# Reordering the Strassen sums of a fused linear-attention and gated-MLP kernel between VectorE and GpSimd

## The chip, the core and the metric

The kernel runs on one core of a Trainium2 chip. The metric is the device time of one launch in microseconds; before the change it is 294.11 us (median of three runs, 294.11 to 294.32). The traced execution spans 292.1 us, and every time of day below ("at 107.95") is microseconds from the start of that span.

The engines are PE (TensorE: matmuls; its weight loads are listed as PEld), DVE (VectorE), ACT (ScalarE), POOL (GpSimd) and SP (which issues the DMAs). Each works through its own queue of instructions strictly in the order of the program, and waits for the others through semaphores.

## What is computed

```
q_s = softmax(q, over head_dim)          # 8 batches, 8 heads, 576 rows, 64 wide
k_s = softmax(k, over the rows)
attn = q_s @ (k_s^T @ v)                 # per head
x = attn, heads side by side             # 4608 x 512
g, val = x @ w_gate, x @ w_val           # 512 -> 1536
out = (gelu(g) * val) @ w_out            # 1536 -> 512, float32
```

## The kernel before

**Blocks.** The work goes through nine blocks of 512 rows: the main rows of batches 0 to 6, then block 8 (the 64 left-over rows of all batches), then block 7. Each block makes `xt` (the attention output, transposed), then `ht` (the hidden rows, `gelu(g)*val`, twelve chunks of 128), then the output product. The attention of the following batch is threaded into the block.

**Two levels of Strassen products.** In blocks 1 and later the output product (`out_strassen`, L755) multiplies `ht` with `w_out` in seven products instead of eight, by way of sums of quarters of `ht`. With `a11, a21, a12, a22` for the quarters (`sum_h`, L576), the four sums are

- 1: `sh[1] = a21 + a22`
- 2: `sh[2] = sh[1] - a11`
- 3: `a21 = a11 - a21`, in place in `ht`
- 4: `s4 = a12 - sh[2]`

Product 5 reads sum 1, product 6 sum 2, product 3 sum 4, product 7 sum 3. `sum_h(j0, j1, which, eng)` does the listed sums for one pair of chunks (`j` = 0, 1 or 2; 128x512 f16) on DVE or on POOL. From block 2 on the first-level products of x with the weights are done the same way for chunks in pairs: `pair_step(b, xt, k, i)` is step `i` (1 to 4) of pair `k`. Step 2 ends with an `add` on DVE (L670), step 3 with another `add` and a `final` (gelu on ACT, multiply on DVE), and `upper` (gelu on ACT, multiply on POOL, L676) closes the pair's other half. Step 4 of a pair accumulates on the bank `pga` that step 3's addition reads. `sum_x` (L613, POOL) makes the sums `xs` of `xt` that these products read. The weights' sums are made once: `sum_wgv` (L595) and, later, chunk by chunk, `sum_w1` (L604).

**What sets the order.** An order written by hand. In blocks 2 and 3 it is the string `FOUR` (L634): `0.1` is step 1 of pair 0, `8g` and `8v` are plain gate and value products of chunk 8 (`half`, L643), and a word such as `s0` or `u0` calls what `plan` has under that name. `s0`/`s1` and `u0`/`u1` are the sums of `ht` for pair 0 and pair 1. `at(b, kind, i, ...)` fills the plan and `ride(b, kind, i)` runs it; `NS` 0 to 4 are places inside `out_strassen`. `u1` is run by `out_strassen` itself, after product 1's fourth chunk (L796). Block 1 has no pairs; its sums for the first four chunks come from `SUMS` (L733), run after the chunk with that number.

**The places that matter.** In `out_strassen`: a snapshot `snap` is a copy of a PSUM bank to SBUF (L775 on ACT, L777 on DVE) that must be taken before the next product accumulates on the same bank; `add` (L783) adds a bank to a snapshot into the output rows. `psa` carries products 1, 6, 7 and 4 in turn, `psc` carries 5 and 3, `psb` carries 2. So product 3 waits for the snapshot of product 5, product 7 for that of product 6, and product 4 for the addition of product 7. After product 6 the attention of the next block is threaded in (`unit_kv4`, L340, and `unit_x4`, L426, whose copies into `xt` are on ACT and DVE).

Of the kernel before, what the change touches and what calls it, by code (L numbers as in the profile page):

```python
# [18 lines left out]
def kernel(  # L19
# [29 lines left out]
    NO = NFI // 2  # L49
# [30 lines left out]
    def big(shape, dt, name, hold=False, seed=False):  # L80
        tag = ring.pop(next(i for i, x in enumerate(ring) if x in full) if seed else 0)
        t = ps_big.tile(shape, dt, name=name, tag=tag)
        words = 1
        for n in shape[1:]:
            words *= n
        (full.add if words == 512 and shape[0] == 128 and dt == f32 else full.discard)(tag)
        if hold:
            held[id(t)] = (t, tag)
        else:
            ring.append(tag)  # L90
        return t

    def let_go(t):
        ring.append(held.pop(id(t))[1])
# [481 lines left out]
    def sum_h(j0, j1, which, eng="dve"):  # L576
        step = 1 if j0 in (0, 4) and j1 < NO + (j0 > 0) else NO // 2
        js, ks = slice(j0, j1, step), slice(NO + j0, NO + j1, step)
        a11, a21 = ht[:, js, 0:256], ht[:, js, 256:512]
        a12, a22 = ht[:, ks, 0:256], ht[:, ks, 256:512]  # L580
        s1, s2 = sh[1][:, js], sh[2][:, js]
        for i in which:
            o, a, b, op = {1: (s1, a21, a22, ALU.add), 2: (s2, s1, a11, ALU.subtract),
                           3: (a21, a11, a21, ALU.subtract),
                           4: (s4[:, js], a12, s2, ALU.subtract)}[i]
            (nc.gpsimd if eng == "pool" else nc.vector).tensor_tensor(out=o, in0=a, in1=b, op=op)  # L586
# [32 lines left out]
    def product_gv(i, ps, xt, k, first):  # L619
        lo, hi = slice(k * P, (k + 1) * P), slice((k + NO // 2) * P, (k + NO // 2 + 1) * P)  # L620
        xs = xs_b[xt is st.get((B - 1, "xt"))]
        for t, w, nm in ((0, wv_sb, "v"), (1, wg_sb, "g")):
# [8 lines left out]

    FOUR = ("a 7g l 7v n 0.1 6.1 0.2 6.2 0.3 6.3 m p 10g 0.4 6.4 1.1 t 10v 1.2 s0 8g u0 1.3 8v 1.4 2.1"  # L634
            " 11g 2.2 11v 2.3 s1")
    FIVE = ("a 8g l 8v n m 0.1 6.1 0.2 6.2 0.3 6.3 0.4 1.1 p 6.4 7.1 t 1.2 7.2 1.3 s0 7.3 2.1 1.4 u0 11g 2.2"
            " y 7.4 11v 2.3 s1")
# [1 line left out]
           " 8.2 2.3 s1 8.3 2.4")  # L639
    steps = {b: (SIX if b >= B - 1 else FIVE if b > 3 else FOUR).split() for b in range(2, B + 1)}  # L640
    live = {}
# [88 lines left out]
            if late:  # L730
                late()

    SUMS = {9: (0, 4, (1, 2)), 10: (0, 4, (3, 4))}  # L733

    def product(i, ps, first, ts=(0, 1), js=range(NO)):
        for j in js:
# [12 lines left out]
    def get_x(b):  # L749
        return get_xt(b) if b < B else xtr  # L750

    def last_js(b):
        return (NO - 2 if b < 2 else NO // 2 - 1, NO)

    def out_strassen(b, last):  # L755
        yo = [yop.tile([P, 2, C], f32, name="yo", tag="yo") for _ in range(2)]
        c = (slice(0, 256), slice(256, 512))
        ps, tiles_ = {}, {}

        def get(nm):  # L760
            if last:
                tiles_[nm] = [big([P, 256], f32, "ps" + nm, True) for _ in range(2)]
                ps[nm] = [x for x in tiles_[nm]]
            else:
                tiles_[nm] = [big([P, 2, 256], f32, "ps" + nm, True)]
                ps[nm] = [tiles_[nm][0][:, t] for t in range(2)]

        def parts(nm):
            return [(0, ps[nm][0]), (1, ps[nm][1])] if last else [(slice(0, 2), tiles_[nm][0])]

        def snap(nm, act=False):
            sn = ffn.tile([P, 2, 256], f32, name="sn", tag="gl")
            for n, (t, src) in enumerate(parts(nm)):
                if n or act:
                    nc.scalar.activation(out=sn[:, t], in_=src, func=ACTF.Copy, scale=1.0 / _H_SCALE)  # L775
                else:
                    nc.vector.tensor_scalar(out=sn[:, t], in0=src, scalar1=1.0 / _H_SCALE,  # L777
                                            scalar2=None, op0=ALU.mult)
            return sn

        def add(nm, sn, half, col):
            for t, src in parts(nm):
                nc.vector.scalar_tensor_tensor(  # L783
                    out=yo[half][:, t, c[col]], in0=src, scalar=1.0 / _H_SCALE,
                    in1=sn[:, t], op0=ALU.mult, op1=ALU.add)

        js = (0, 1, 2, 3, 4, 5) if b < 2 else (0, 3, 1, 4, 2, 5)
        get("a")
        four = 1 < b < B - 1
        cut = 3 if four else 4  # L790
        product(1, ps["a"], True, js=js[:cut])
        if four:
            pair_step(b, get_x(b), NO // 2 - 1, 4)
            product(1, ps["a"], False, js=js[cut:4])
        ride(b, NS, 0)
        if b < 4:  # L796
            ride(b, PR, "u1")
        if b >= B - 1:
            pair_step(b, get_x(b), NFI - NO // 2 - 1, 4)
        get("b")  # L800
        product(1, ps["a"], False, js=js[4:])
        if b > 1:
            s1 = snap("a", True)
        ride(b, PR, "e")
        sum_h(*last_js(b), (1,))
        if b > 3:
            ride(b, PR, "u1")
        sum_h(*last_js(b), (2,))
        if b < 2:
            s1 = snap("a")  # L810
        product(2, ps["b"], True, js=js)
        add("b", s1, 0, 0)
        for x in tiles_["b"]:
            let_go(x)
        sum_h(*last_js(b), (4,), "pool" if b > 1 else "dve")
        get("c")
        product(5, ps["c"], True, js=js)
        sum_h(*last_js(b), (3,), "pool" if b > 1 else "dve")
        s5 = snap("c", b == B or b == B - 2)
        ride(b, NS, 1)  # L820
        product(6, ps["a"], False, js=js)
        s2 = snap("a", b == B or b == B - 2)
        ride(b, NS, 2)
        cut = NO - 1 if 1 < b < B - 2 else NO
        product(3, ps["c"], False, js=js[:cut])
        if cut < NO:
            product(7, ps["a"], False, js=js)
            add("a", s5, 1, 1)
            product(3, ps["c"], False, js=js[cut:])
        add("c", s2, 0, 1)  # L830
        for x in tiles_["c"]:
            let_go(x)
        store_rows(b, 0, yo[0])
        if last:
            finish_last(b, ps["a"], yo[1], s5)
            return
        if cut == NO:
            product(7, ps["a"], False, js=js)
            add("a", s5, 1, 1)
        ride(b, NS, 4)  # L840
        if b == B:
            go_on(B - 1, get_x(B - 1), 1)
        product(4, ps["a"], False, js=js)
        nc.scalar.activation(out=yo[1][:, :, c[0]], in_=tiles_["a"][0], func=ACTF.Copy,
                             scale=1.0 / _H_SCALE)
        let_go(tiles_["a"][0])
        store_rows(b, 1, yo[1])
# [16 lines left out]
    def store_rows(b, half, yo):  # L864
        if b < B:
            store(nc.sync, yo.rearrange("p n c -> p (n c)"), b, 2 * half, 2 * half + 2)
            return
        for t in range(2):
            for j in range(2):
                o = 2 * (2 * half + t) + j  # L870
                nc.sync.dma_start(
                    out=out[o * S:(o + 1) * S, :].rearrange("(m n) c -> m n c", n=NT)[:, 0, :],
                    in_=yo[j * 64:(j + 1) * 64, t, :])
# [71 lines left out]
    FI, NS, PR = range(3)  # L945
    plan = {}

    def at(b, kind, i, *fns):
        plan.setdefault((b, kind, i), []).extend(fns)

    L = lambda f, *a: (lambda: f(*a))
# [35 lines left out]
    for i, x in enumerate(("g1", "v1", "g2", "v2", "g4", "v4")):  # L987
        at(0, FI, 5 + i, L(sum_wgv, x[0], int(x[1])))
    at(0, FI, NFI - 2, L(sum_w, 1))
    at(1, NS, 1, L(sum_wgv, "g", 3))  # L990
    at(1, NS, 2, L(sum_wgv, "v", 3))
    for b in range(2, B):
        n = b + 1
        if n < B:
# [13 lines left out]
    for b in range(2, B - 1):  # L1008
        n = b + 1
# [6 lines left out]
    for b in range(2, B + 1):  # L1016
        for j in range(NO // 2 - 1):
            at(b, PR, f"s{j}", L(sum_h, j, NO, (1,)))
            if j and b > 3:
                at(b, PR, f"u{j}", L(sum_h, j, NO, (2, 3, 4)))  # L1020
            else:
                at(b, PR, f"s{j}", L(sum_h, j, NO, (3,), "pool"))
                at(b, PR, f"u{j}", L(sum_h, j, NO, (2,)), L(sum_h, j, NO, (4,), "pool"))
    for b, kind, i, dk, x in ((1, FI, 6, 0, 1), (1, FI, 6, 0, 2), (1, FI, 6, 0, 4), (1, FI, 9, 0, 3),
                              (2, NS, 1, 1, 1), (2, NS, 1, 1, 2), (3, NS, 2, 1, 4), (3, NS, 2, 1, 3),
                              (4, NS, 2, 2, 1), (4, NS, 2, 2, 2), (6, NS, 1, 2, 4), (6, NS, 2, 2, 3)):
        at(b, kind, i, L(sum_w1, x, NO + dk, "pool" if b < 3 else "dve"))


    def ride(b, kind, i):  # L1030
        for fn in plan.get((b, kind, i), []):
            fn()

    for b in order:
# [11 lines left out]
        for fi in range(fi0, NFI if b < 2 else 0):  # L1046
            ffn_fi(xt, fi, b == 1 and fi == 7)
            ride(b, FI, fi)
            if b > 0 and fi in SUMS:
                sum_h(*SUMS[fi])  # L1050
        if b == 0:
# [44 lines left out]
```

The softmax here doesn't subtract the row's maximum and nothing guards it: scores larger than these inputs give would overflow.

## Time and profile before

| view | what it says |
|---|---|
| page, busy time | PE 281.8 us, 96% of the span; DVE 78%, POOL 69%, ACT 68% |
| page, clock | TensorE's granted clock is at 9 or more tenths in every slice |
| chain that ended last | 87% of the span on PE, 4% DVE, 4% POOL |
| sums of h on DVE (L586), groups by shape | 22 of `sh<-sh,ht` at a mean of 603 ns; 22 of `sh<-ht` at 441 ns; six of `s<-ht,sh` at 418 ns |
| sums of h on POOL (L586) | 16 of `ht<-ht` at 1197 ns, 16 of `s<-ht,sh` at 1172 ns |
| chunk sums of the weights (L611) | POOL 1156 to 1602 ns, DVE 916 and 1150 ns |
| blocks in the trace | block 1's output product 70.7 to 82.2; block 2 from 82.2, its output product 101 to 112.6; block 3 from 112.6, its output product 132.2 to 143.8; block 4 from 143.8 |

A matmul is pipelined: one of 256 columns lasts 272 ns in the records, but twelve in a row leave PE after 1.31 us, 0.109 us each, and four of 512 columns after 0.86 us. PE's lost time is therefore read from the starts: where a group of matmuls begins, plus its number times this pitch, is where the next could begin. The idle time in square brackets in a timeline is shorter than that loss, because it is counted from the modelled end of the last matmul.

### The profile page before, as it was taken

The page shows a single profiled execution, that of the slowest core. Times are in us where ns is not written, and L with a number is a line of the kernel's source. Part 1 is how long each engine was busy: PE and PEld are TensorE (multiplying, and loading weights), DVE is VectorE, ACT ScalarE, POOL GpSimd, SP SyncE. Part 2 cuts the span into 40 slices and gives each one's busy share as a digit, 9 for nine tenths or more (in the row PEclk, how much of TensorE's full clock was granted, in tenths as well). Part 3 has the DMA queues.
Part 4 walks back from the last instruction along what each step waited for, and adds up shares of the span by engine and source line. Part 5 has one row for each costly group of instructions (what it writes and reads, how often), then busy time and mean ns, then how long its engine had stood idle before and what let it go on. Part 6 is the DMA issues. An engine that isn't in the chain of part 4 may idle for free.

```text
span 292.1 us, 6496 instructions
## 1 busy us (share of the span) xinstructions
PE 281.8 (96%) x2497; PEld 207.5 (71%) x2497; DVE 229.2 (78%) x426; ACT 198.1 (68%) x332; POOL 200.2 (69%) x184
## 2 busy tenths in 40 slices
PE   3999999999999999999999999999999999999994
PEld 1444445445777786768688878887888888888883
DVE  2954888868997678669988889887889779938992
ACT  3763367785697688766887698769774477537650
POOL 1567746986478589976996689759975476283640
PEclk9999999999999999999999999999999999999999
DMA  6999999998059903990189318921240110033003
GB/s 217 374 381 388 400 392 390 354 342 236 3 165 375 183 2 137 345 239 2 72 271 323 74 74 274 312 67 53 93 83 19 72 75 0 3 73 73 2 0 144
DMA packets 54622, 51.72 MB, mean 177 GB/s; under 512 B 18496, under 2 KB 50496, under 8 KB 54592
## 3 DMA queue, kind: packets, MB, share of 16 engines
q1 hardware_dynamic: 52864, 49.49, 54.1%
q10 hardware_dynamic: 1728, 1.84, 1.9%
q8 instruction: 19, 0.31, 0.4%
q14 instruction: 11, 0.09, 0.1%
HBM read 37.75 MB, written 9.44 MB: 162 GB/s over the span
## 4 chain that ended last, share of the span: by engine, by line
PE 87%; DVE 4%; POOL 4%; DMA 2%; ACT 1%; issue 1%; POOLq 0%; ACTq 0%
PE pga L629 21%; PE psa L745 12%; PE psg L471 11%; PE psv L471 10%; PE pgc L629 10%; PE psc L745 6%; PE pgb L629 5%; PE psy L539 4%; PE psb L745 2%; DMA qt<-in_q_dram 2%; DVE sh L586 2%; PE pskv L347 2%; POOL s L586 1%; POOL v L186 1%; PE psx L434 1%
## 5 line engine op out<-in xcount | busy, mean ns | idle before, releaser
L629 PEld LDWEIGHTS <-wgv_sb 128*128 128x128 f16 x560 | 54.3, 98 | 11.2 <-issue 0.8
L471 PEld LDWEIGHTS <-wgv_sb 128*128 128x128 f16 x304 | 29.5, 98 | 30.3 <-issue 0.7
L248 POOL TENSOR_TENSOR eq<-eq,rrq 128x640 f16<-128x640 f16 (+1 forms) x27 | 34.8, 1306 | 11.3 <-DVE rrq L240 7.3
L745 PEld LDWEIGHTS <-ht 128*128 128x128 f16 x384 | 36.6, 98 | 7.8 <-issue 2.5
L471 PE MATMUL psg<-xt,wgv_sb 128*128 128x512 f16 x152 | 41.1, 379 | 0.0
L471 PE MATMUL psv<-xt,wgv_sb 128*128 128x512 f16 x152 | 41.0, 379 | 0.0
L676 POOL TENSOR_TENSOR ht<-eq 128x512 f16<-128x512 f32 x17 | 21.7, 1274 | 22.4 <-ACT eq L674 22.4
L629 PE MATMUL pga<-xs,wgv_sb 128*128 128x256 f16 x232 | 34.5, 272 | 0.2 <-DVE cc L670 0.2
L586 POOL TENSOR_TENSOR s<-ht,sh 128x512 f16<-128x512 f16 x16 | 18.7, 1172 | 13.9 <-DVE sh L586 13.9
L656 ACT ACTIVATE glq<-pgb 128x256 f32<-128x256 f32 x35 | 13.3, 381 | 21.1 <-PE pgb L629 14.4
L657 DVE SCALAR_TENSOR_TENSOR ht<-pga,glq 128x256 f16<-128x256 f32 x35 | 14.8, 422 | 14.2 <-ACT glq L656 14.0
L586 POOL TENSOR_TENSOR ht<-ht 128x512 f16<-128x512 f16 x16 | 19.2, 1197 | 8.7 <-DVE sh L586 8.7
L476 ACT ACTIVATE gl<-psg 128x512 f32<-128x512 f32 x24 | 13.8, 598 | 16.6 <-PE psg L471 16.5
L186 POOL CAST v<-vt 128x640 f16<-128x640 f32 x26 | 19.1, 777 | 8.1 <-PE pskv L347 6.4
L477 DVE SCALAR_TENSOR_TENSOR ht<-psv,gl 128x512 f16<-128x512 f32 x24 | 16.0, 686 | 10.0 <-PE psv L471 8.2
L686 ACT COPY pgb<-pga 128x512 f32<-128x512 f32 x35 | 20.4, 582 | 5.1 <-PE pga L629 4.8
L745 PE MATMUL psa<-tw,ht 128*128 128x256 f16 x192 | 23.4, 272 | 0.1
L666 ACT ACTIVATE snq<-pga 128x512 f32<-128x512 f32 x35 | 20.9, 600 | 3.5 <-PE pga L629 3.2
L210 ACT ACTIVATE ek<-kt 128x1280 f16<-128x1280 f32 (+1 forms) x11 | 19.1, 1748 | 6.1 <-DMA kt<-in_k_dram 4.2
L676 POOL TENSOR_TENSOR ht<-cc 128x512 f16<-128x512 f32 x16 | 20.4, 1272 | 2.8 <-ACT cc L674 2.8
L238 DVE TENSOR_REDUCE rq<-eq 128x20 f32<-128x1280 f16 (+1 forms) x12 | 17.2, 1432 | 4.4 <-ACT eq L210 4.4
L745 PEld LDWEIGHTS <-sh 128*128 128x128 f16 x192 | 18.7, 98 | 2.3
(173 smaller groups left out, 685.2 us busy)
## 6 DMA issues: line engine op xcount, KB each, us to landing
out_dram<-yo SPq DMA_DIRECT2D x15, 512.0 KB, 3.4
kt<-in_k_dram SPq DMA_DIRECT2D x7, 640.0 KB, 9.0
vt<-in_v_dram SPq DMA_DIRECT2D x7, 640.0 KB, 5.9
qt<-in_q_dram SPq DMA_DIRECT2D x7, 640.0 KB, 7.7
qt<-in_q_dram SPq DMA_DIRECT2D x8, 512.0 KB, 8.4
wost<-in_moe_w_out_dram SPq DMA_DIRECT2D x6, 512.0 KB, 7.9
kt<-in_k_dram SPq DMA_DIRECT2D x6, 512.0 KB, 9.6
vt<-in_v_dram SPq DMA_DIRECT2D x6, 512.0 KB, 6.5
```

Of the source, the lines that this page charges most:

```text
L186: nc.gpsimd.tensor_copy(out=dst, in_=src)
L210: nc.scalar.activation(out=dst[:, n0:NC, h0 * D:h1 * D].rearrange(o, d=D, **({"t": 2} if b >= QUAD else {})), in_=heads(tiles[(nm, b)], b, ...
L238: nc.vector.reduce_sum(rq, e, axis=mybir.AxisListType.X)
L248: (nc.gpsimd if eng == "pool" else nc.vector).tensor_tensor(out=e, in0=e, in1=rrq.unsqueeze(-1).to_broadcast((P, n, 2, D)), op=ALU.mult)
L471: nc.tensor.matmul(ps, w[:, ci, fi * P:(fi + 1) * P], xt[:, ci, :], start=(ci == 0), stop=(ci == HP - 1))
L477: nc.vector.scalar_tensor_tensor(out=ht[:, fi, :], in0=psv, scalar=_H_SCALE, in1=gl, op0=ALU.mult, op1=ALU.mult)
L586: (nc.gpsimd if eng == "pool" else nc.vector).tensor_tensor(out=o, in0=a, in1=b, op=op)
L629: nc.tensor.matmul(ps[:, t], a, x, start=(first and t == 0 and c == 0), stop=(c == 1), skip_group_check=True)
L666: nc.scalar.activation(out=sn, in_=ps, func=ACTF.Copy, scale=_H_SCALE)
L676: (nc.vector if k == NFI - NO // 2 - 1 else nc.gpsimd).tensor_tensor(out=ht[:, k:k + NO // 2 + 1:NO // 2, 256:512], in0=cc[:, :, 0], in1=c ...
L686: nc.scalar.copy(out=pb, in_=pa)
L745: nc.tensor.matmul(ps[t], a, w, start=(first and j == js[0] and (t == ts[0] or ps[t].tensor is not ps[ts[0]].tensor)), stop=(j == js[-1]), ...
```

## The change

It moves sums, and adds or removes none. There are five edits.

1. In `FOUR` (blocks 2 and 3) the word `s0` moves from ahead of `8g 1.3` to behind them, and `u0` from ahead of `1.3` to behind `8v`. Pair 0's sums on DVE then stand behind step 1.3's addition. The order of the matmuls stays.
2. In blocks 2 and 3 pair 1's sum 4 goes from POOL to DVE (in `u1`, next to sum 2), and pair 1's sum 3 stays on POOL but is queued later, under the new name `r1`, behind pair 2's sum 4.
3. In block 1 sum 4 of chunks 0 to 3 moves from after chunk 10 to after chunk 11, so that it stands behind chunk 11's multiply on DVE.
4. In block 1 the weights' sum `g3` moves from the place after product 5 to the place after product 6, beside `v3`, so that both stand behind the second snapshot.
5. In block 2 two chunk sums of the weights go from POOL to DVE, and from the place after product 5 to the place after product 6.

Its aim is to free PE's short waits at the addition of step 1.3, at the snapshots and at `xs`.

```diff
-    FOUR = ("... 6.4 1.1 t 10v 1.2 s0 8g u0 1.3 8v 1.4 2.1"
+    FOUR = ("... 6.4 1.1 t 10v 1.2 8g 1.3 s0 8v u0 1.4 2.1"
             " 11g 2.2 11v 2.3 s1")
...
-    SUMS = {9: (0, 4, (1, 2)), 10: (0, 4, (3, 4))}
+    SUMS = {9: (0, 4, (1, 2)), 10: (0, 4, (3,)), 11: (0, 4, (4,))}
...
         sum_h(*last_js(b), (4,), "pool" if b > 1 else "dve")
+        ride(b, PR, "r1")
         get("c")
         product(5, ps["c"], True, js=js)
...
-    at(1, NS, 1, L(sum_wgv, "g", 3))
-    at(1, NS, 2, L(sum_wgv, "v", 3))
+    at(1, NS, 2, L(sum_wgv, "g", 3), L(sum_wgv, "v", 3))
...
             else:
-                at(b, PR, f"s{j}", L(sum_h, j, NO, (3,), "pool"))
-                at(b, PR, f"u{j}", L(sum_h, j, NO, (2,)), L(sum_h, j, NO, (4,), "pool"))
+                if j:
+                    at(b, PR, "r1", L(sum_h, j, NO, (3,), "pool"))
+                    at(b, PR, "u1", L(sum_h, j, NO, (2, 4)))
+                else:
+                    at(b, PR, "s0", L(sum_h, j, NO, (3,), "pool"))
+                    at(b, PR, "u0", L(sum_h, j, NO, (2,)), L(sum_h, j, NO, (4,), "pool"))
...
-                              (2, NS, 1, 1, 1), (2, NS, 1, 1, 2), (3, NS, 2, 1, 4), (3, NS, 2, 1, 3),
+                              (2, NS, 2, 1, 1), (2, NS, 2, 1, 2), (3, NS, 2, 1, 4), (3, NS, 2, 1, 3),
...
-        at(b, kind, i, L(sum_w1, x, NO + dk, "pool" if b < 3 else "dve"))
+        at(b, kind, i, L(sum_w1, x, NO + dk, "pool" if b < 2 else "dve"))
```

More of the change, by code (lines that the diff above doesn't have):

```diff
@@ L630, in product_gv @@
                                  skip_group_check=True)
-    FOUR = ("a 7g l 7v n 0.1 6.1 0.2 6.2 0.3 6.3 m p 10g 0.4 6.4 1.1 t 10v 1.2 s0 8g u0 1.3 8v 1.4 2.1"
+    FOUR = ("a 7g l 7v n 0.1 6.1 0.2 6.2 0.3 6.3 m p 10g 0.4 6.4 1.1 t 10v 1.2 8g 1.3 s0 8v u0 1.4 2.1"
             " 11g 2.2 11v 2.3 s1")
```

## The prediction

> **What bounds the kernel now.** I read the page first, then PE's waits, then the timeline around each.
>
> ```profile
> PE 281.8 (96%) x2497; PEld 207.5 (71%) x2497; DVE 229.2 (78%) x426; ACT 198.1 (68%) x332; POOL 200.2 (69%) x184
> PE 87%; DVE 4%; POOL 4%; DMA 2%; ACT 1%; issue 1%; POOLq 0%; ACTq 0%
> ```
>
> PE is the bound: 96% busy, 87% of the chain. No edit removes a matmul, so all that can be won is time in which PE stands still. The view of PE's waits names where:
>
> ```profile
> PE psc L745 <- POOL s L586: 0.5, 2, 0.3
> PE pgc L629 <- POOL xs L617: 0.3, 1, 0.3
> PE pga L629 <- DVE cc L670: 0.2, 1, 0.2
> PE psb L745 <- DVE ht L477: 0.2, 1, 0.2
> ```
>
> These count from a modelled end, so I take the losses from starts: group start, plus 0.109 us for each 256-column matmul (0.216 for 512), against the next start. Three stretches of the timeline carry the argument. The addition of step 1.3, block 3:
>
> ```profile
> 125.45 0.83 DVE L586 TENSOR_TENSOR sh<-ht 128x512 f16<-128x512 f16 x1
> 126.12 1.03 PE L471 MATMUL psv<-xt,wgv_sb 128*128 128x512 f16 x4
> 126.31 0.42 DVE L586 TENSOR_TENSOR sh<-sh,ht 128x512 f16<-128x512 f16 x1
> 126.66 0.68 DVE L670 SCALAR_TENSOR_TENSOR cc<-pga,snq 128x512 f32<-128x512 f32 x1
> 127.39 0.60 PE L629 MATMUL pga<-xs,wgv_sb 128*128 128x256 f16 x4 [0.24 <-DVE cc L670]
> ```
>
> PE is free at 126.12 + 4 x 0.216 = 126.98 and starts at 127.39, 0.05 behind the end of the addition (127.34): 0.41 lost. The addition's product had started at 125.25 and ended at 125.85; it waited for two sums. Block 2 has the same at 96.20 (free at 95.22 + 0.86): 0.12.
>
> The end of block 2:
>
> ```profile
> 103.63 1.15 POOL L586 TENSOR_TENSOR ht<-ht 128x512 f16<-128x512 f16 x1
> 103.83 1.24 DVE L586 TENSOR_TENSOR sh<-sh,ht 128x512 f16<-128x512 f16 x1
> 105.15 1.27 POOL L586 TENSOR_TENSOR s<-ht,sh 128x512 f16<-128x512 f16 x1 [0.36 <-DVE sh L586]
> 105.44 1.26 DVE L586 TENSOR_TENSOR sh<-sh,ht 128x512 f16<-128x512 f16 x1
> 106.22 1.47 PE L745 MATMUL psa<-tw,sh 128*128 128x256 f16 x12
> 106.78 1.16 POOL L586 TENSOR_TENSOR s<-ht,sh 128x512 f16<-128x512 f16 x1 [0.36 <-DVE sh L586]
> 107.23 0.67 DVE L777 TENSOR_SCALAR sn<-psc 128x512 f32<-128x512 f32 x1
> 107.95 1.25 PE L745 MATMUL psc<-wo_sb,s 128*128 128x256 f16 x10 [0.26 <-POOL s L586]
> ```
>
> PE is free at 106.22 + 1.31 = 107.53, product 3 starts at 107.95: 0.42 lost. The view blames POOL's sum, but that ends at 107.94, 0.01 ahead; the snapshot of `psc` ends at 107.90, 0.05 ahead, the distance seen above. I hold the snapshot to be the releaser. It is late because two DVE sums of 0.42 took 1.24 and 1.26: each began under a POOL sum and ended 0.28 after it (104.78 to 105.07; 106.42 to 106.70). Block 3 repeats this (139.14, free at 138.72): 0.42.
>
> The start of block 3: `pgc` starts at 115.24, though PE is free at 114.36 + 0.44 = 114.80: 0.44 lost, for `xs`, which POOL begins at 114.02 behind
>
> ```profile
> 110.25 1.16 POOL L611 TENSOR_TENSOR sh<-tw,wgv_sb 128x512 f16<-128x512 f16 x1
> 111.35 2.72 POOL L186 CAST v<-vt 128x640 f16<-128x640 f32 x4
> ```
>
> Block 1 loses 0.33 at 73.46 (`psb` behind chunk 11's multiply), 0.14 at 78.61 (product 7 behind a snapshot that stood behind a weight sum) and 0.10 at 80.86 beyond what every block shows there.
>
> **What the skill says.** The Trainium skill, "SBUF — State Buffer", section "SBUF: two separate sides", says that DVE and POOL share a pair of ports as an exclusive lock: a DVE instruction with two SBUF inputs and a POOL instruction that reads SBUF exclude each other for a whole instruction, the first to start winning. The trace agrees: the sums that took 1.24 and 1.26 ended 0.28 after POOL's, while a sum alone has 0.42. "GPSIMD Engine Reference", section "4.1 Engine selection", has POOL about twice as slow for two-input operations; here it is 1.16 against 0.42, nearer three times.
>
> **The change, part by part.**
>
> *Edit 1, sums of pair 0.* In block 3 the addition can start when its product is out, at 125.9, and ends at 126.6, ahead of PE's 126.98. Gain 0.41, and 0.12 in block 2 by the same sum. Sums 1 and 2 now stand on DVE between the `final` of 1.3 and the `final` of 1.4. What is queued behind them: the multiply of `8v`, then 1.4's `final` (129.91 before, ahead of which DVE was idle 1.65). Sum 1 takes 0.42 from about 127.1; sum 2 starts at about 128.1 and may be locked out by `upper` on POOL (1.27, from about 127.4), so it ends at 129.0 at worst, while 1.4's multiply isn't due before 129.5. POOL's own two sums slide behind `upper` and end at about 131, inside its idle 3.5 ahead of 133.59. Cost nothing.
>
> *Edit 2, pair 1.* In block 2 sum 2 starts at about 103.85 with POOL idle from 103.68 (`upper`, from 102.41, 1.27): ends 104.3 and not 105.07. Sum 4 follows on DVE: 0.42 if alone, 1.24 if locked out; POOL has nothing to do until pair 2's sum 2, so I take 0.42, to 104.7. Pair 2's sums 1 and 2 end at 105.1 and 105.5 (before: 106.70). The addition to `psb` then ends at 106.2. Product 5 is out at 106.4, so the snapshot of `psc` ends at 107.1, 0.4 ahead of PE's 107.53. Gain 0.42 in block 2 and 0.42 in block 3. POOL now has sum 4 of pair 2 (105.55 to 106.75), then sum 3 of pair 1 (to 107.9) and of pair 2 (to 109.05). Product 7, which starts at 107.53 + 10 x 0.109 = 108.62, takes its chunks in the order 0, 3, 1, 4, 2, 5: pair 1 at 109.06, pair 2 at 109.49. Slack 1.1 and 0.4. That PE waits by chunk and not for the last sum is seen in block 2 before, where product 7 started at 109.04 and the last sum ended at 109.06.
>
> *Edit 5, weights' chunk sums.* POOL loses 2.3 us (two of 1.16) ahead of the casts, so `xs` could begin near 112 and waits only for `xt`; block 3's own end, where these sums are on DVE already, has no wait at the matching place. Gain 0.44. DVE gets two sums behind the second snapshot. Block 3 shows their price there: 139.61 to 141.38, 1.77 us, both in conflict with POOL; alone they would be 2 x 0.42. Snapshot 2 runs in block 2 from 107.73 to 108.41, so they end between 109.2 and 110.15. Behind them on DVE is the addition of product 7, due at 110.13, and for that waits product 4 on PE, then the copies into `xt`. At the dear end this costs 0 to 0.1, in blocks 2 and 3 both, since the same slack shrinks in block 3 (there from 0.36). I take 0.07 each.
>
> *Edits 3 and 4, block 1.* DVE has no pause longer than 0.1 from 67.55 to 84, so here DVE and not PE sets the pace: PE's two waits are its queue. With sum 4 behind chunk 11's multiply, `psb` no longer waits (ready at 72.86, due at 73.13), but the snapshot ahead of product 6 moves only by the pauses for a result just made that the new order fills, 73.44 to 73.32. So product 6 comes at 74.87 and not 75.00: 0.12. Edit 4 lets product 7 start earlier, but the total of DVE work ahead of product 7's addition is unchanged, and PE waits at product 4 instead. Together 0.12; the far end, if all of the block's waits went, is 0.57.
>
> **Sum.** 0.41 + 0.12 + 2 x 0.42 + 0.44 + 0.12 = 1.93, less 2 x 0.07 = 1.79. 294.11 - 1.79 = 292.3.
>
> **The rivals.**
>
> A. *The waits are only handed on.* Edit 5's sums hold DVE, or POOL's late sum 3 holds product 7, in each of blocks 2 and 3. For it: DVE and POOL are packed there, and each lock-out is worth 0.8. Against it: the slacks above. Half of the two 0.42s and of the 0.44 is left: 0.53 + 0.42 + 0.22 - 0.2 = about 1.0, so 293.1.
>
> B. *All of block 1's waits go too* and nothing is paid back: 1.81 + 0.57 = 2.4, so 291.7. Against it: DVE's unbroken queue.
>
> C. *No gain.* What PE wins is lost at the next block's start, where the last copy into `xt` was only just in time (PE waited 0.03 at 144.47). That copy follows the same chain, so it should move with PE. 294.1.
>
> D. *Slower.* The moved sums meet POOL's in new places; each DVE sum that is locked out costs 0.8 on a queue that PE waits for. Two in block 2 and two in block 3, of which half reaches PE, with only the 0.53 of edit 1 kept: +1.6 - 0.5 = +1.1, so 295.2. Against it: POOL idles while pair 1's sums run.
>
> **How the numbers follow.** The forecast 0.70; A 0.12; B 0.05; C 0.08; D 0.05. The range must hold the forecast, A and most of B: 291.7 to 293.3 leaves out C and D and a little of B, about 0.15. Faster by over 0.59 us: 0.87; within it: 0.08; slower: 0.05.
>
> **What would show it.** In the changed trace: no PE wait at `pgc` for `xs` at block 3's start; pair 1's `sh<-sh,ht` in blocks 2 and 3 near 0.42 and not 1.24; the snapshot of `psc` ending ahead of PE's last matmul of product 6; step 1.4 of pair 1 following `8v` without a pause; in block 1 PE's wait at `psb` gone and one of nearly its length at product 6. I am wrong if product 4 starts over 0.2 later behind product 7's addition than before, or if product 7 waits for POOL.

## The result, and the profile after

The changed kernel takes 292.15 us (median of four runs, 292.11 to 292.29) against 294.22 us of the kernel before on the same chip: 2.07 us less, a ratio of 0.993 with a 95% interval of 0.9913 to 0.9948. Forecast: 292.3.

The page of the changed kernel, engines and chain:

```profile
PE 281.3 (97%) x2497; PEld 207.4 (71%) x2497; DVE 229.4 (79%) x430; ACT 197.8 (68%) x332; POOL 195.1 (67%) x180
PE 95%; DVE 2%; ACTq 1%; ACT 1%; issue 0%
```

POOL gave four instructions to DVE (184 to 180, 426 to 430). POOL is gone from the chain, which ran through it for 4% before. In the view of PE's waits the four lines shown before are gone; only the one at the start of the kernel is left:

```profile
PE pswarm L463 <- ACT warm L892: 4.9, 1, 4.9
```

That doesn't mean that PE waits nowhere: the view counts from modelled ends and misses short waits, so the losses are read from starts again. From trace to trace the whole time line is shifted by up to 0.28 us at block 0 already (its first gate product starts at 14.96 before and at 15.03 to 15.24 in most of the others), where no edit reaches. I therefore compare lengths: from the start of product 2 (`psb`) in one block to its start in the next.

| from product 2 of block | before | after | gain |
|---|---|---|---|
| 1 to 2 | 31.56 | 31.27 | 0.29 |
| 2 to 3 | 31.19 | 29.93 | 1.26 |
| 3 to 4 | 30.05 | 29.62 | 0.43 |
| 4 to 5 | 29.62 | 29.63 | 0 |
| sum of the first three | 92.80 | 90.82 | 1.98 |

The 29.6 us of the untouched block 4 are what blocks 2 and 3 now come close to.

**Step 1.3's addition, block 3**, in the timeline of the changed kernel (start in us, duration, engine, line, operation, out<-in with shapes, count, and in brackets idle time and its releaser):

```profile
124.90 0.69 DVE L670 SCALAR_TENSOR_TENSOR cc<-pga,snq 128x512 f32<-128x512 f32 x1 [0.36 <-PE pga L629]
126.00 0.60 PE L629 MATMUL pga<-xs,wgv_sb 128*128 128x256 f16 x4
126.14 0.41 DVE L586 TENSOR_TENSOR sh<-ht 128x512 f16<-128x512 f16 x1
126.39 1.29 POOL L676 TENSOR_TENSOR ht<-cc 128x512 f16<-128x512 f32 x1 [1.71 <-ACT cc L674]
127.08 0.89 DVE L586 TENSOR_TENSOR sh<-sh,ht 128x512 f16<-128x512 f16 x1
128.52 0.43 DVE L657 SCALAR_TENSOR_TENSOR ht<-pga,glq 128x256 f16<-128x256 f32 x1 [0.56 <-ACT glq L656]
```

The addition ends at 125.59 and step 1.4 starts at 126.00, where PE is free (`8v`'s four matmuls began at 125.14). Sum 2 began under `upper` and ended 0.29 behind it (127.68 to 127.97), as the prediction's dear end had it, and DVE still idled 0.56 ahead of 1.4's multiply.

**The end of block 2**, timeline of the changed kernel:

```profile
103.69 0.42 DVE L586 TENSOR_TENSOR sh<-sh,ht 128x512 f16<-128x512 f16 x1
104.14 0.42 DVE L586 TENSOR_TENSOR s<-ht,sh 128x512 f16<-128x512 f16 x1
104.94 0.42 DVE L586 TENSOR_TENSOR sh<-sh,ht 128x512 f16<-128x512 f16 x1
105.44 1.16 POOL L586 TENSOR_TENSOR s<-ht,sh 128x512 f16<-128x512 f16 x1 [1.90 <-DVE sh L586]
106.09 1.47 PE L745 MATMUL psa<-tw,sh 128*128 128x256 f16 x12
106.29 0.69 DVE L777 TENSOR_SCALAR sn<-psc 128x512 f32<-128x512 f32 x1 [0.33 <-PE psc L745]
107.40 1.26 PE L745 MATMUL psc<-wo_sb,s 128*128 128x256 f16 x10
108.21 0.91 DVE L611 TENSOR_TENSOR tw<-wgv_sb 128x512 f16<-128x512 f16 x1
109.15 0.82 DVE L611 TENSOR_TENSOR sh<-tw,wgv_sb 128x512 f16<-128x512 f16 x1
110.00 0.69 DVE L783 SCALAR_TENSOR_TENSOR yo<-psa,sn 128x512 f32<-128x512 f32 x1
```

All of DVE's sums take 0.42. The snapshot of `psc` ends at 106.98, 0.42 ahead of product 3 at 107.40, which is 106.09 + 1.31. The two chunk sums of the weights end at 109.97, and the addition of product 7 starts at 110.00, 0.04 behind the end of its product: just in time. Block 3 shows the same picture.

**The start of block 3**, timeline of the changed kernel:

```profile
111.85 1.15 POOL L617 TENSOR_TENSOR xs<-xt 128x512 f16<-128x512 f16 x1
114.25 0.38 PE L629 MATMUL pgc<-xs,wsv 128*128 128x256 f16 x2
```

`xs` begins at 111.85 in place of 114.02 and is done 1.25 us ahead of `pgc`, which follows the four matmuls of `pga` (from 113.81) without a wait. In the kernel before it waited:

```profile
115.24 0.38 PE L629 MATMUL pgc<-xs,wsv 128*128 128x256 f16 x2 [0.28 <-POOL xs L617]
```

**Block 1** still waits, in new places. First the wait at `psb` in the timeline of the kernel before, then the timeline of the changed kernel:

```profile
73.46 0.39 PE L745 MATMUL psb<-wo_sb,ht 128*128 128x256 f16 x2 [0.16 <-DVE ht L477]
```

```profile
73.51 1.47 PE L745 MATMUL psc<-tw,sh 128*128 128x256 f16 x12
74.25 0.68 DVE L777 TENSOR_SCALAR sn<-psa 128x512 f32<-128x512 f32 x1
74.99 1.48 PE L745 MATMUL psa<-tw,sh 128*128 128x256 f16 x12
80.85 1.47 PE L745 MATMUL psa<-tw,ht 128*128 128x256 f16 x12
```

`psb` no longer waits for chunk 11's multiply, but product 6 starts at 74.99 and not at 73.51 + 1.31 = 74.82: 0.17 for the snapshot, which ends at 74.93. Product 4's loss grew from 0.20 to 0.31 us.

### The profile page after: what moved, and what is told of

It is laid out like the page before. It is cut to its first block, busy times and chain, and to the rows that moved or that the text cites. A ratio compares the mean times of both kernels' runs of the same rounds, so it can differ in the third digit from the quotient of the medians.

```text
span 290.3 us, 6495 instructions
## 1 busy us (share of the span) xinstructions
PE 281.3 (97%) x2497; PEld 207.4 (71%) x2497; DVE 229.4 (79%) x430; ACT 197.8 (68%) x332; POOL 195.1 (67%) x180
## 4 chain that ended last, share of the span: by engine, by line
PE 95%; DVE 2%; ACTq 1%; ACT 1%; issue 0%
PE pga L629 21%; PE psa L745 14%; PE psg L471 11%; PE psv L471 11%; PE pgc L629 11%; PE psc L745 7%; PE pgb L629 5%; PE psb L745 4%; PE psy L539 4%; PE pswarm L463 2%; PE pskv L347 1%; PE psx L434 1%; ACTq L166 1%; DVE yo L783 1%; PE pst L372 1%; PE psx L413 1%
## 5 line engine op out<-in xcount | busy, mean ns | idle before, releaser
L586 POOL TENSOR_TENSOR s<-ht,sh 128x512 f16<-128x512 f16 x14 | 16.2, 1155 | 16.3 <-DVE sh L586 16.3
```

## The experiments

e1 to e4 put one edit, or one pair, into the kernel before; the others vary the changed kernel. Each time is a median, and each ratio is to the kernel before on the same chip, whose own median was 294.15 to 294.22 us. "PE loss" is read from starts as above.

| kernel | time, us | ratio to before, 95% interval |
|---|---|---|
| the change | 292.15 | 0.9930 (0.9913 to 0.9948) |
| e1: edit 1 alone | 293.64 | 0.9982 (0.9975 to 0.9990) |
| e2: edit 2 alone | 293.45 | 0.9976 (0.9966 to 0.9986) |
| e3: edit 5 alone | 293.60 | 0.9980 (0.9973 to 0.9987) |
| e4: edits 3 and 4 alone | 294.06 | 0.9995 (0.9987 to 1.0003) |
| f1: chunk sums ahead of snapshot 2 | 293.52 | 0.9976 (0.9967 to 0.9985) |
| f2: pair 1's sum 3 early on POOL | 292.34 | 0.9937 (0.9924 to 0.9950) |
| f4: pair 2's sum 4 twice | 294.19 | 0.9999 (0.9990 to 1.0007) |
| g3: the change without edit 1 | 292.31 | 0.9938 (0.9924 to 0.9951) |
| f3: block 1's chunk sums moved | 291.98 | 0.9925 (0.9912 to 0.9938) |
| g2: g3 and v3 moved | 291.90 | 0.9925 (0.9912 to 0.9937) |
| g1: both of these | 291.76 | 0.9918 (0.9905 to 0.9932) |
| h1: g1, product 3 split in blocks 1 and 6 | 292.75 | 0.9952 (0.9939 to 0.9966) |

The intervals of f2, f3, g1, g2 and g3 overlap with that of the change, and the chips differ by up to 0.07 us, so the small differences between these kernels rest on the traces. From product 2 of block 1 to that of block 4 the changed kernel takes 90.82 us; f2 takes 0.27 more, g3 0.21 more, f3 0.12 less, g2 0.19 less and g1 0.28 less. Such a length is that of one execution; for e2 and e3 it differs from the medians by 0.2 us, in opposite directions.

### Each edit alone

**e1, edit 1.**

```diff
-    ... t 10v 1.2 s0 8g u0 1.3 8v 1.4 2.1
+    ... t 10v 1.2 8g 1.3 s0 8v u0 1.4 2.1
```

> The kernel before with edit 1 alone (pair 0's sums behind step 1.3's addition in blocks 2 and 3). Theory (each edit frees its own PE wait, independently): the losses of 0.12 and 0.41 us at step 1.4 go, the four others stay: -0.53 us, so about 293.7. Rival (the edits only work together, because a wait freed in a block comes back at the next wait of the same block, which is bound by DVE or POOL): block 2's and block 3's ends then lose more than 0.42 each and the time falls by 0.1 us at most.

Measured: -0.54 us. The losses of 0.12 and 0.41 at step 1.4 are gone, the others stand (0.42, 0.43 and 0.42). As the theory had it.

**e2, edit 2.**

```diff
         sum_h(*last_js(b), (4,), "pool" if b > 1 else "dve")
+        ride(b, PR, "r1")
...
-                at(b, PR, f"s{j}", L(sum_h, j, NO, (3,), "pool"))
-                at(b, PR, f"u{j}", L(sum_h, j, NO, (2,)), L(sum_h, j, NO, (4,), "pool"))
+                if j:
+                    at(b, PR, "r1", L(sum_h, j, NO, (3,), "pool"))
+                    at(b, PR, "u1", L(sum_h, j, NO, (2, 4)))
...
```

> The kernel before with edit 2 alone (pair 1's sum 4 on DVE, its sum 3 on POOL behind pair 2's sum 4). Theory: pair 1's sums on DVE take 0.42 and not 1.24 us, the snapshot ahead of product 3 is early, both losses of 0.42 go: -0.84 us, so about 293.4; but POOL's chunk sums of the weights stay in block 2, so the loss at xs grows by what PE wins ahead of it unless POOL too gets its sums done earlier: then only -0.42 to -0.5. Rival (the edits only work together): under -0.2 us.

Measured: -0.73 us by the times, -0.56 by the lengths in the traces. Both waits at product 3 are gone, but the wait at `pgc` grew from 0.44 to 0.74 us. Timeline of e2:

```profile
110.22 1.16 POOL L611 TENSOR_TENSOR sh<-tw,wgv_sb 128x512 f16<-128x512 f16 x1
111.32 2.71 POOL L186 CAST v<-vt 128x640 f16<-128x640 f32 x4
114.00 1.15 POOL L617 TENSOR_TENSOR xs<-xt 128x512 f16<-128x512 f16 x1
115.20 0.38 PE L629 MATMUL pgc<-xs,wsv 128*128 128x256 f16 x2 [0.59 <-POOL xs L617]
```

POOL's sums, casts and `xs` stand where they stood before (110.25, 111.35, 114.02): of the 0.42 that PE won ahead of it in block 2, 0.30 was lost again in waiting for POOL. The caution in the expectation was right; the forecast of the prediction counted this edit with edit 5 in place.

**e3, edit 5.**

```diff
-    (2, NS, 1, 1, 1), (2, NS, 1, 1, 2), ...      "pool" if b < 3 else "dve"
+    (2, NS, 2, 1, 1), (2, NS, 2, 1, 2), ...      "pool" if b < 2 else "dve"
```

> The kernel before with edit 5 alone (two chunk sums of the weights from POOL to DVE, behind block 2's second snapshot). Theory: POOL reaches xs 2.3 us earlier, the loss of 0.44 us at the start of block 3 goes and nothing else changes: -0.44 us, so about 293.8. Rival (DVE is now as late as POOL was): product 4 waits for DVE's addition instead, 0 to -0.2 us.

Measured: -0.58 us by the times, -0.79 by the lengths. More than expected: the wait at `pgc` is gone, and the one at step 1.4 in block 3 fell from 0.41 to 0.09, though edit 1 isn't in. Timeline of e3:

```profile
122.97 2.49 POOL L248 TENSOR_TENSOR eq<-eq,rrq 128x640 f16<-128x640 f16 x2
125.22 0.52 DVE L586 TENSOR_TENSOR sh<-ht 128x512 f16<-128x512 f16 x1
126.11 0.68 DVE L670 SCALAR_TENSOR_TENSOR cc<-pga,snq 128x512 f32<-128x512 f32 x1
126.84 0.60 PE L629 MATMUL pga<-xs,wgv_sb 128*128 128x256 f16 x4
```

Pair 0's sum 1 takes 0.52 and not 0.83: it ends 0.28 behind POOL's normalisation of the next `eq`, and POOL gets there 0.54 earlier in the trace, while the sum itself starts only 0.23 earlier. In the kernel before POOL had no pause from 107.90 to 126.00, so work put on its queue at 109 still delayed it at 123. POOL's two chunk sums had cost PE twice, 12 us apart.

**e4, edits 3 and 4.**

```diff
-    SUMS = {9: (0, 4, (1, 2)), 10: (0, 4, (3, 4))}
+    SUMS = {9: (0, 4, (1, 2)), 10: (0, 4, (3,)), 11: (0, 4, (4,))}
...
-    at(1, NS, 1, L(sum_wgv, "g", 3))
-    at(1, NS, 2, L(sum_wgv, "v", 3))
+    at(1, NS, 2, L(sum_wgv, "g", 3), L(sum_wgv, "v", 3))
```

> The kernel before with edits 3 and 4 alone (block 1). Theory (DVE's unbroken queue sets the pace of block 1's end): PE's wait at psb goes and comes back at product 6 and at product 4; the block gets 0.1 to 0.2 us shorter. Rival (the waits were PE's own and go): -0.57 us.

Measured: -0.12 us, with an interval of the ratio that includes 1; by the losses -0.17. The waits at `psb` (0.32) and product 7 (0.13) are gone, product 6 now waits 0.17 and product 4 waits 0.31 where it waited 0.20. The waits were moved more than removed; the rival is out. The two edits were not run apart.

**g3, the change without edit 1.** The overlap seen in e3 asks what edit 1 is worth beside edit 5.

```diff
-    ... t 10v 1.2 8g 1.3 s0 8v u0 1.4 2.1
+    ... t 10v 1.2 s0 8g u0 1.3 8v 1.4 2.1
```

> The changed kernel without edit 1. Edit 5 alone had, beside the wait for xs, taken 0.32 of the 0.40 us at step 1.4 in block 3 with it, because POOL was ahead and pair 0's sum 1 on DVE was locked out for less. Theory (edits 1 and 5 share that wait): with all other edits in, edit 1 is worth only 0.12 in block 2 and 0.09 in block 3: +0.2 us, so about 292.35. Rival (they are worth what each was alone): +0.53, so about 292.7.

Measured: 292.31, +0.16 us. PE loses 0.12 in block 2 and 0.08 in block 3. Edit 1 alone was worth 0.54, as the last of the edits 0.16 to 0.20.

### What makes the sums wait, and what waits for them

**f1, the chunk sums ahead of the snapshot.**

```diff
-    (2, NS, 2, 1, 1), (2, NS, 2, 1, 2)
+    (2, NS, 1, 1, 1), (2, NS, 1, 1, 2)
```

> The changed kernel with edit 5's two chunk sums on DVE, but ahead of block 2's second snapshot instead of behind it. Theory (what stands behind the snapshot matters, because product 7 waits for it): the sums run from about 106.9 to 108.7, the snapshot ends near 109.3 and product 7, due at 108.5, starts about 0.9 us late; part of that comes back, since the addition of product 7 no longer stands behind the sums: +0.8 to +0.9 us, so about 293.0. Rival (only the change of engine matters): no change, 292.15.

Measured: 293.52, +1.37 us. Timeline of f1:

```profile
106.48 2.45 POOL L586 TENSOR_TENSOR ht<-ht 128x512 f16<-128x512 f16 x2
106.83 1.09 DVE L611 TENSOR_TENSOR tw<-wgv_sb 128x512 f16<-128x512 f16 x1
107.95 1.26 DVE L611 TENSOR_TENSOR sh<-tw,wgv_sb 128x512 f16<-128x512 f16 x1
109.14 0.68 DVE L777 TENSOR_SCALAR sn<-psa 128x512 f32<-128x512 f32 x1
109.87 1.47 PE L745 MATMUL psa<-tw,ht 128*128 128x256 f16 x12 [1.28 <-DVE sn L777]
```

Here the sums meet POOL's two sums 3, take 2.35 us together instead of 1.8, and product 7 starts 1.45 us late (due at 107.33 + 10 x 0.109 = 108.42). The engine is the same as in the changed kernel, so the place decides; and the size was under-estimated: I had taken 1.8 us for the two, a price from another neighbour. One after the other they take 0.91 and 0.82 in the changed kernel, 1.09 and 1.26 here, and 0.47 and 0.82 in f2 below.

**f2, pair 1's sum 3 early on POOL.**

```diff
-    at(b, PR, "r1", L(sum_h, j, NO, (3,), "pool"))
+    at(b, PR, "s1", L(sum_h, j, NO, (3,), "pool"))
```

> The changed kernel with pair 1's sum 3 on POOL at its old place, right behind pair 1's sum 1 (s1), in blocks 2 and 3; sum 4 stays on DVE. Theory (DVE's sums are locked out while POOL runs a sum): POOL runs sum 3 from about 103.55 to 104.7, pair 1's sum 2 on DVE takes up to 1.24 us instead of 0.42 and all behind it slides by about 0.7; the snapshot of psc, which has 0.42 us of slack, ends about 0.2 us too late: +0.2 us in each of the two blocks, or none if the other sums run free. Rival (it was the move of sum 4 off POOL that mattered, the order on POOL doesn't): pair 1's sum 2 stays at 0.42 us and the time at 292.15.

Measured: 292.34, +0.19 us. Timeline of f2:

```profile
103.30 1.15 POOL L586 TENSOR_TENSOR ht<-ht 128x512 f16<-128x512 f16 x1
103.49 1.24 DVE L586 TENSOR_TENSOR sh<-sh,ht 128x512 f16<-128x512 f16 x1
105.11 0.42 DVE L586 TENSOR_TENSOR sh<-ht 128x512 f16<-128x512 f16 x1
```

With nothing but the order on POOL changed, the same sum takes 1.24 us in place of 0.42: 0.28 past the end of POOL's. That is the lock-out, shown alone. But PE pays elsewhere than I expected: product 5 stalls 0.14 in its middle for pair 2's sum 1 (ends 105.53, PE goes on at 105.58), and 0.13 in block 3, and product 3 starts without a wait. So of the 0.42 that edit 2 wins per block, about 0.14 hang on the order of POOL's queue. The rest, 0.28, is there in f2 too: it comes with sum 4's move to DVE, which ends the other lock-out (pair 2's sum 2 takes 0.42 in f2). What the order alone would win, with sum 4 left on POOL, was not run.

**f4, pair 2's sum 4 done twice.**

```diff
         sum_h(*last_js(b), (4,), "pool" if b > 1 else "dve")
+        if b in (2, 3):
+            sum_h(*last_js(b), (4,), "pool")
```

> The changed kernel with pair 2's sum 4 done twice on POOL in blocks 2 and 3 (same result). It asks what released product 3 in the kernel before. Theory (the snapshot of psc; the sums are waited for chunk by chunk): the second sum 4 ends near 107.75, but product 3 still starts at 107.4, when PE is free; product 7 comes to POOL's sum 3 of pair 2 about 0.65 us too early in the middle of its twelve matmuls and waits there, and xs is about 1.2 us later. Rival (POOL's sum 4, as the view of waits had it): product 3 starts only behind it, at about 107.8, 0.35 to 0.4 us late in each of the two blocks. Time +1.3 to +2 us either way; the places of the waits decide.

Measured: 294.19, +2.04 us. Timeline of f4:

```profile
105.41 2.39 POOL L586 TENSOR_TENSOR s<-ht,sh 128x512 f16<-128x512 f16 x2 [1.89 <-DVE sh L586]
106.26 0.69 DVE L777 TENSOR_SCALAR sn<-psc 128x512 f32<-128x512 f32 x1 [0.33 <-PE psc L745]
107.37 1.26 PE L745 MATMUL psc<-wo_sb,s 128*128 128x256 f16 x10
107.75 2.45 POOL L586 TENSOR_TENSOR ht<-ht 128x512 f16<-128x512 f16 x2
110.26 0.61 PE L745 MATMUL psa<-tw,ht 128*128 128x256 f16 x4 [0.68 <-POOL ht L586]
```

POOL writes the sum until 107.80, and product 3 starts at 107.37 all the same, where PE is free (106.06 + 1.31). So its first matmul doesn't wait for pair 2's sum 4, the sum that the view of waits names. That leaves the snapshot, which ended 0.05 ahead of product 3 in the kernel before. Product 7 then stops twice, for 0.07 ahead of pair 1's chunks and for 0.86 ahead of pair 2's: the sums are waited for chunk by chunk.

### Block 1

**f3, block 1's chunk sums out of the way.**

```diff
-    (1, FI, 6, 0, 1), (1, FI, 6, 0, 2), (1, FI, 6, 0, 4), (1, FI, 9, 0, 3)
+    (1, FI, 7, 0, 1), (1, FI, 8, 0, 2), (1, FI, 8, 0, 4), (1, NS, 2, 0, 3)
...
-        ... "pool" if b < 2 else "dve"
+        ... "pool" if b < 2 and x == 3 else "dve"
```

> The changed kernel with block 1's four chunk sums of the weights taken out of the way of DVE's sums of h: sums 1, 2 and 4 go to DVE, into its idle stretches behind chunks 7 and 8, and sum 3 goes to POOL behind block 1's casts. Theory (DVE's queue sets the pace of block 1's end, and its two first sums, 1.14 and 1.52 us, are long because POOL runs chunk sums then): they fall to 0.68 each, DVE runs 1.3 us earlier, PE's waits at product 6 (0.17) and at product 4 (0.2 beyond the usual) go: -0.3 to -0.37 us, so about 291.8. Rival (the waits come from the chain of products and snapshots, not from DVE's queue): under -0.1 us.

Measured: 291.98, -0.17 us by the times and -0.12 by the lengths: half of the forecast or less. Timeline of f3:

```profile
68.44 0.69 DVE L586 TENSOR_TENSOR sh<-ht 128x1024 f16<-128x1024 f16 x1
69.17 0.69 DVE L586 TENSOR_TENSOR sh<-sh,ht 128x1024 f16<-128x1024 f16 x1
73.17 0.68 DVE L777 TENSOR_SCALAR sn<-psa 128x512 f32<-128x512 f32 x1
77.65 1.83 DVE L602 TENSOR_TENSOR wgv_sb<-wgv_sb 128x768 f16<-128x768 f16 x2
80.01 0.67 DVE L783 SCALAR_TENSOR_TENSOR yo<-psa,sn 128x512 f32<-128x512 f32 x1
80.74 1.47 PE L745 MATMUL psa<-tw,ht 128*128 128x256 f16 x12 [0.21 <-DVE yo L783]
```

The two first sums fall from 1.14 and 1.52 to 0.69 each, DVE runs 1.08 us earlier (snapshot at 73.17, in the changed kernel at 74.25), and product 6's wait is gone. But at 77.65 DVE comes to `g3` and `v3`, which run beside POOL's casts and take 1.83 together (0.54 is the shorter of the two in g2), and the lead is lost: product 4 waits 0.37.

**g2, only g3 and v3 moved, and g1, both.**

```diff
-    at(1, NS, 2, L(sum_wgv, "g", 3), L(sum_wgv, "v", 3))
+    at(1, FI, 6, L(sum_wgv, "g", 3))
+    at(1, FI, 7, L(sum_wgv, "v", 3))
```

> The changed kernel with g3 and v3 moved behind chunks 6 and 7 only; the four chunk sums stay on POOL, where they lock out the two first sums of h. Theory: DVE's late start costs product 6 its 0.17 us, or more, since g3 and v3 now also stand ahead of it, but product 4's wait falls to 0.1 us: 0 to -0.2 us, so 292.0 to 292.15. Rival (DVE's total work is what counts, wherever it stands): 292.15.

Measured: 291.90, -0.25 us: a little more than expected. Product 6 waits 0.08, product 4 waits 0.195.

> f3_relief and, on top, block 1's weight sums g3 and v3 moved from the place after product 6 to the places behind chunks 6 and 7 on DVE. Theory (in f3_relief product 4 waits because g3 and v3, locked out by the casts, take 1.8 us on DVE between the snapshot of product 6 and the additions): without them the additions follow their products and product 4 waits only the 0.1 us that it waits in blocks 2 to 5: -0.27 us against f3_relief, so about 291.7. Rival (the wait comes from the products' own chain): as f3_relief, about 292.0.

Measured: 291.76, -0.39 us against the change. Product 6 has no wait, product 4 waits 0.195: not the 0.1 that I had foreseen. Neither moved work on DVE can lower it; DVE idles 0.62 us ahead of the addition now.

**h1, product 3 split in blocks 1 and 6**, on top of g1.

```diff
-        cut = NO - 1 if 1 < b < B - 2 else NO
+        cut = NO - 1 if 0 < b < B - 1 else NO
```

> g1_relief_both, and the last two of product 3's twelve matmuls are done after product 7 in blocks 1 and 6 as well, as blocks 2 to 5 have it. It asks what product 4's wait of 0.195 us in block 1 is, which the prediction had counted as 0.10 too long. Theory (it is the chain product 7, addition, product 4, with two matmuls too few to fill it): it falls by 0.1 in blocks 1 and 6, -0.2 us, so about 291.55. Rival (product 7 then starts 0.22 us earlier and waits for the snapshot of product 6 or for POOL): the wait moves to product 7, no change, 291.76.

Measured: 292.75, +0.99 us against g1; both expectations missed. Product 4's wait did fall, from 0.195 to 0.09 in both blocks, so it was the chain of product 7, addition and product 4. But PE lost more elsewhere. The split turns the two additions round on DVE: `yo<-psc`, which ran under product 7 in g1, now stands between product 7's addition and the copies into `xt` and `xtr`, and the next block waits for those. Timeline of h1:

```profile
79.46 0.69 DVE L783 SCALAR_TENSOR_TENSOR yo<-psa,sn 128x512 f32<-128x512 f32 x1 [1.86 <-PE psa L745]
80.07 0.68 DVE L783 SCALAR_TENSOR_TENSOR yo<-psc,sn 128x512 f32<-128x512 f32 x1
81.42 1.29 DVE L190 CAST xt<-psx 128x512 f16<-128x512 f32 x2
82.76 0.38 PE L471 MATMUL psg<-xt,wgv_sb 128*128 128x512 f16 x1 [0.22 <-DVE xt L190]
231.98 0.38 PE L629 MATMUL pgc<-xs,wsv 128*128 128x256 f16 x2 [0.45 <-POOL xs L617]
```

PE loses 0.47 us at the start of block 2 (0.09 and 0.38). In block 8 it loses 0.61 (0.08 in the kernel before) for `xs`, which is made from `xtr`, and 0.21 at 237.00, where it waits for a DVE addition that ends at 236.95. g1, at 291.76, is the fastest of all versions.

## Why the prediction was right, point by point

The forecast was a gain of 1.79 us; the times give 2.07, the lengths in the traces 1.98.

| step of the prediction | forecast | in the trace |
|---|---|---|
| edit 1, blocks 2 and 3 | 0.12 + 0.41 | 0.12 + 0.41 |
| edit 2, product 3 in blocks 2 and 3 | 2 x 0.42 | 2 x 0.42 |
| edit 5, `xs` | 0.44 | 0.44 |
| edit 5, DVE behind the snapshot | -2 x 0.07 | 0 |
| edits 3 and 4, block 1 | 0.12 | 0.17 |

The last two rows, 0.14 and 0.05, are the whole difference between 1.79 and 1.98.

- **Edit 1**: right, with the lock-out under `upper` that it allowed for. As a price of the edit alone, e1 agrees; beside edit 5 it is 0.08 in block 3 (g3). The prediction summed the two as if they were independent. The sum came out right, because each loss was counted once, but the credit for 0.32 of block 3's 0.41 belongs to either edit.
- **Edit 2**: right in its times: POOL idle, sums of 0.42, snapshot 0.4 ahead of PE. That POOL's sum was not the releaser is shown by f4, which leaves the snapshot; that DVE's long sums were a lock-out by POOL, by f2.
- **Edit 5**: right at `xs`. The 2 x 0.07 were the dear end of a range of 0 to 0.1; the sums ended 0.03 ahead of the addition that waits for them, so the cost is nothing, but there is no slack left either. f1 shows what the same two sums cost at the wrong place: 1.37 us.
- **Edits 3 and 4**: the reading "handed on" is right (e4). With the shift of 0.16 between the two traces taken off, product 6 starts at 74.83 (forecast 74.87) and product 4 0.17 earlier than before (forecast 0.12). The wait at product 6 is 0.17, though: half of the 0.33 that was at `psb`, not "nearly its length". One term was mis-read: the prediction counted 0.10 of product 4's wait in the kernel before as DVE's. h1 shows that all of its 0.195 is the chain of product 7, addition and product 4, in a block that doesn't split product 3. After the change 0.11 more is DVE's, and g2 takes that away. "DVE sets the pace" holds in two places, the first sums of h (f3) and `g3` with `v3` (g2); only both together leave PE no wait for DVE's queue (g1).
- **The rivals**: A's two ways didn't occur: the addition starts 0.04 behind product 7's end, and product 7 starts at 108.49, where PE is free. A wait that is handed on is seen in e2, at another place (`pgc`), because only edit 5 made room on POOL. B (291.7) is nearly what g1 reaches, but with other moves than this change. C and D have no support in the trace of the change. What D feared, DVE sums that meet POOL's ahead of something PE waits for, is what f1 does; h1 loses time at the very copies into `xt` that C had named.

## What to carry to other kernels

Where two engines share a lock, look at the durations of the same instruction and not only at its waits: a sum that takes 0.42 and in places 1.24 tells whom it met, and moving the neighbour is as good as moving the sum. Place work on a queue by what stands behind it: the same two sums cost nothing behind a snapshot and 1.37 us ahead of it, and an order that frees one wait (h1) may put a short instruction ahead of what the next stage needs. Price edits together as well as singly: here edit 2 alone lost over a third of its gain to the next wait, and edits 1 and 5 removed the same wait.

## What the runs showed of the hardware

- The Trainium skill, "SBUF — State Buffer", section "SBUF: two separate sides", has the lock between DVE and POOL held for a whole instruction. f2 agrees: the blocked sum waits for the whole rest of POOL's instruction and ends 0.28 to 0.29 us behind it, in f2 (104.45 to 104.73), in e3 (125.46 to 125.74) and under `upper` in the changed kernel (127.68 to 127.97).
- New to me was how such a lock-out travels: taking two sums off POOL in e3 made a DVE sum 0.31 us shorter some 14 us later, in a stage that the edit didn't touch.
- A packed POOL queue did not keep DVE out for longer than one instruction. In f1 POOL ran two sums in a row (106.48 to 107.63 and 107.60 to 108.93), and each of DVE's two sums was held by one of them only: they ended at 107.92 and 109.21, 0.29 and 0.28 behind. POOL's second sum then took 1.33 us in place of 1.15.
- The view of waits put product 3's wait down to POOL's sum, which ended last of its releasers in the record; the real one ended 0.04 earlier and stood 0.05 ahead of the matmul. A distance of 0.05 from a releaser's end to the start behind it recurs in these traces (127.34 to 127.39, 105.53 to 105.58), and tells the two apart here; f4 agrees.
